# One weight load on all partitions, another gate and new planner constants in a fused attention and mixer kernel

## The chip, the core and the metric

The kernel runs on one core of one Trainium2 chip. Its engines have these names in the profile: PE is TensorE (matrix products), DVE is VectorE, ACT is ScalarE, POOL is GpSimd, and SP is SyncE, which here only starts transfers. Sixteen DMA engines move data between memory and the core. The metric is the device time of one execution in microseconds (us). A profiled execution shows a span, which is 1.7 to 1.9 us shorter than the time of the same execution; differences between spans are comparable with differences between times. Landings of transfers are taken from the landing records of a trace and stand 0.05 us later than the same events in the views.

One execution can differ from the next: each run lists the mean clock that was granted to PE, and a run that is over 1.5% longer than the fastest of its kernel is called slow and left out of comparisons. Ratios below are the mean time of one kernel's fast runs over the mean of the other's fast runs of the same rounds, so they are not quite the ratio of the medians that stand beside them. An interval in brackets is a 95% interval.

## The reference

The task is a gated linear attention, followed by a token mixing and a channel mixing layer, for 4 batches of 768 tokens with 8 heads of 48 (so 384 channels).

```python
# attention: per batch and head
f = 1.0 / (1.0 + np.exp(-f_logit))
for t in range(S):
    state = f[:, :, t, :, None] * state + np.einsum('bhd,bhe->bhde', k[:, :, t], v[:, :, t])
    y[:, :, t] = np.einsum('bhd,bhde->bhe', q[:, :, t], state)
# x = y with the heads side by side: (4, 768, 384)
xt = x.transpose(0, 2, 1)
h = np.maximum(xt @ w_tok1, 0.0) @ w_tok2      # (768, 256), (256, 768): token weights
u = x + h.transpose(0, 2, 1)
h2 = np.maximum(u @ w_ch1, 0.0) @ w_ch2        # (384, 1536), (1536, 384): channel weights
return u + h2
```

All inputs and the output are float32 in memory; the kernel multiplies in bf16.

## The kernel before

Each batch is treated in three parts of 256 tokens. A part is named by batch and number: "v of part 1,0" is the v data of batch 1, part 0. The program doesn't issue its instructions in the order in which they are written. A planner in the kernel file takes a list of operations with assumed durations, simulates the engines, and so fixes the order on each engine when the program is built. The assumed duration of a transfer is `xfer`. It never changes what a transfer costs on the chip, only the order that the planner chooses:

```python
            end = st + occ + lat
            if o.xfer is not None and e == "POOL":
                sw = max(st + occ + 1.5, sw) + o.xfer      # transfers that POOL starts
                pipe = max(pipe, st + occ) + o.xfer
                end = sw + 1.0
            elif o.xfer is not None:                       # transfers that SP starts
                pipe = max(st + occ + 0.9, pipe) + o.xfer
                # ... (cut)
```

The first token weight comes in four transfers of 64 partitions; two casts make it bf16. The channel weights are transferred by POOL, in halves a and b each. A gate is a tiny POOL copy that reads another load's data, so that the transfer behind it starts only when that load has landed:

```python
    gates = dict(zip(("wc1a", "wc1b", "wc2a", "wc2b"), ("w2s1", "-", "k1,1", "-")))
    # ...
        if at_ != "-":
            P.op(f"gate_{nm}", {"POOL": (0.13, 0.1)}, [at_], [],
                 lambda: nc.gpsimd.tensor_copy(gate_t, P[at_][:, 0, 0, 0:1]), -900 + len(sw), dep)
    # ...
    w1v = moe_w_tok1.rearrange("(kt p two) n -> two p kt n", p=64, two=2)
    # ...
    for n in range(2):
        def w1ld(n=n):
            for j in range(2):
                nc.sync.dma_start(out=flat(f"w1s{n}")[64 * j:64 * j + 64].rearrange("p (kt c) -> p kt c", c=DT),
                                  in_=w1v[j, :, 3 * n:3 * n + 3])
        P.op(f"w1l{n}", {"SP": (1.2, 0)}, [], [f"w1s{n}"], w1ld, -400 + n, [tail], xfer=0.393 / 0.35)
        # ... then one cast of 128x768 for each n, on POOL or ACT
```

Behind the token weights in SP's queue follow the loads of batch 1. The channel products are `ch1` (line L777, the first channel weight) and `ch2` (line L802, the second); in the changed kernel, and in kernels built from it without further lines, the same lines are L776 and L801. Filler matmuls (L858, later L857) on a dummy tile stand in PE's program before 40 us to keep PE busy while it would wait.

## Time and profile before

| quantity | before |
|---|---|
| time, median of three runs | 189.42 us (189.19 to 190.62) |
| span of the profiled run, clock | 186.9 us, 0.977 |
| PE busy | 173.3 us, 93% |
| PE at half clock, start excepted | 24.84 to 31.66 us, and from 185.3 us to the end |
| first channel matmul (L777) starts | 42.54 us |
| PE idle from 45 to 70 us | 25.00 - 22.94 = 2.06 us |
| PE idle from 70 to 140 us | 70.00 - 69.21 = 0.79 us |

The table is read in this way. PE is the bound, so the time can be cut up by PE alone: when the channel products begin, and how much PE stands idle after that. The last two rows come from the view that sums each engine's busy time over stretches. These are its rows for the kernel before. The columns are the stretch and its length, then for PE, PEld, DVE, ACT and POOL the busy time with the number of instructions, then the granted clock, the DMA share and the GB/s moved.

```profile
20.00:24.00 4.00, 3.26 (x94) 1.99 (x93) 2.88 (x6) 1.46 (x4) 2.81 (x3) 1.00 1.12 227
...
45.00:70.00 25.00, 22.94 (x336) 14.48 (x337) 17.50 (x32) 18.11 (x35) 11.31 (x17) 1.00 1.07 224
70.00:140.00 70.00, 69.21 (x941) 42.58 (x938) 46.95 (x85) 45.60 (x87) 25.90 (x39) 1.00 0.96 182
```

The last figure of the first row will matter: while the half loads of the first token weight began to move, the DMA engines delivered 227 GB/s.

### The profile page before, as it was taken

The numbers are of one execution on the slowest core, as the hardware profiler recorded it, in microseconds if no ns is written. First come the engines' busy times: TensorE is split into PE (matmuls) and PEld (weight loads), VectorE is DVE, ScalarE is ACT, GpSimd is POOL, SyncE is SP. The second block draws the span as 40 slices with busy tenths as digits, with TensorE's granted clock in tenths as the row PEclk, the third lists the DMA queues.
The fourth block names the chain that finished last, engine by engine and source line by source line (L and its number), as shares of the span: only waits on it lengthen the run. The fifth ranks groups of instructions, "written<-read, shape, count | busy, mean of one in ns | idle before, by whom it ended". The sixth has DMA issues, their size and how long they took to land.

```text
span 186.9 us, 5369 instructions
## 1 busy us (share of the span) xinstructions
PE 173.3 (93%) x2218; PEld 106.3 (57%) x2224; DVE 111.0 (59%) x213; ACT 117.3 (63%) x214; POOL 60.4 (32%) x97
## 2 busy tenths in 40 slices
PE   6699879999998799999999999999999999999990
PEld 2345555665566466666556655666557566665550
DVE  6389747699676487388866473979447173112021
ACT  3878479699988079578974854649516650833900
POOL 3017644373763311554562453024301130000000
PEclk9999966999999999999999999999999999999998
DMA  6999999999999979999999999305970003303033
GB/s 147 261 261 264 240 277 206 209 256 249 260 224 212 241 180 255 121 291 290 193 243 182 162 296 188 96 4 119 135 142 4 4 0 84 84 4 84 0 86 84
DMA packets 69592, 31.01 MB, mean 166 GB/s; under 512 B 63168, under 2 KB 69312, under 8 KB 69568
## 3 DMA queue, kind: packets, MB, share of 16 engines
q1 hardware_dynamic: 67200, 28.32, 73.0%
q0 software_dynamic: 2368, 2.36, 7.6%
q8 instruction: 17, 0.28, 0.6%
q14 instruction: 7, 0.06, 0.1%
HBM read 25.17 MB, written 4.72 MB: 160 GB/s over the span
## 4 chain that ended last, share of the span: by engine, by line
PE 69%; DMA 13%; ACT 6%; DVE 6%; issue 2%; POOL 2%; POOLq 0%; DVEq 0%; ACTq 0%
PE pp L802 24%; PE pp L777 20%; DMA w_ch<-in_moe_w_ch_dram 6%; PE pp L714 5%; DMA v_ld<-in_v_dram 4%; PE pp L730 3%; PE pp L662 3%; PE pp L674 3%; PE pp L645 3%; DMA f_ld<-in_f_logit_dram 2%; PE pp L858 2%; PE pp L600 2%; PE pp L751 2%; DVE xu L736 2%; DVE AmT L652 1%
## 5 line engine op out<-in xcount | busy, mean ns | idle before, releaser
L802 PE MATMUL pp<-w_ch,zT 128*128 128x384 bf16 x288 | 51.1, 326 | 1.9 <-DMA w_ch<-in_moe_w_ch_dram 1.9
L777 PE MATMUL pp<-uT,w_ch 128*128 128x384 bf16 x288 | 52.3, 326 | 0.2 <-ACT zT L784 0.2
L784 ACT ACTIVATE zT<-pp 128x384 bf16<-128x384 f32 x75 | 35.8, 492 | 21.6 <-PE pp L777 15.3
L802 PEld LDWEIGHTS <-zT 128*128 128x128 bf16 x288 | 27.1, 98 | 19.1 <-issue 2.1
L777 PEld LDWEIGHTS <-w_ch 128*128 128x128 bf16 x288 | 26.4, 98 | 16.9 <-issue 0.4
L812 DVE TENSOR_TENSOR xu<-xu,pp 128x384 f32<-128x384 f32 x24 | 13.2, 550 | 30.7 <-PE pp L802 30.7
L652 DVE TENSOR_TENSOR AmT<-pp,msk 128x1024 bf16<-128x1024 f32 x24 | 28.5, 1217 | 4.7 <-PE pp L645 3.4
L440 POOL CAST x_bf<-xu 128x768 bf16<-128x768 f32 x10 | 8.3, 829 | 29.5 <-ACT xu L698 29.5
L858 PE MATMUL pp<-idle 128*128 128x512 bf16 (+7 forms) x58 | 15.6, 382 | 2.2 <-DVE idle L340 1.5
L786 DVE TENSOR_SCALAR zT<-pp 128x384 bf16<-128x384 f32 x21 | 11.3, 553 | 7.4 <-PE pp L777 7.2
L557 POOL TENSOR_TENSOR qkh<-q_ld,G 128x384 bf16<-128x384 f32 x14 | 12.6, 914 | 7.2 <-ACT G L535 4.3
L440 POOL CAST v_bf<-v_ld 128x768 bf16<-128x768 f32 x10 | 8.3, 826 | 16.6 <-DMA v_ld<-in_v_dram 13.8
L494 ACT ACTIVATE f_ld<-f_ld 128x768 f32<-128x768 f32 x12 | 10.1, 838 | 5.6 <-DMA f_ld<-in_f_logit_dram 5.6
L501 DVE TENSOR_TENSOR Pf<-f_ld 128x384 f32<-128x384 f32 x12 | 7.1, 592 | 8.6 <-ACT f_ld L496 7.7
L698 ACT COPY xu<-pp 128x768 f32<-128x768 f32 x11 | 8.8, 798 | 5.3 <-PE pp L662 4.0
L736 DVE TENSOR_TENSOR xu<-xu,pp 128x384 f32<-128x384 f32 x24 | 11.5, 546 | 0.3 <-PE pp L730 0.2
L557 DVE TENSOR_TENSOR qkh<-k_ld,pp 128x384 bf16<-128x384 f32 x22 | 11.3, 546 | 0.6 <-ACT pp L537 0.6
L506 POOL TENSOR_TENSOR Plo<-Pf,Phi 128x384 bf16<-128x384 f32 x10 | 9.5, 946 | 5.4 <-ACT Phi L438 5.0
L645 PE MATMUL pp<-qkT 48*64 48x128 bf16 x384 | 9.9, 225 | 1.0 <-ACT qkT L438 0.4
L524 DVE TENSOR_TENSOR pp<-pp,f_ld 128x384 f32<-128x384 f32 x12 | 6.8, 563 | 6.9 <-PE pp L520 4.2
L535 ACT ACTIVATE G<-pp 128x768 bf16<-128x768 f32 x12 | 9.7, 808 | 1.2 <-DVE pp L524 1.0
L496 ACT ACTIVATE f_ld<-f_ld 128x768 f32<-128x768 f32 x12 | 10.2, 848 | 0.1
(83 smaller groups left out, 228.5 us busy)
## 6 DMA issues: line engine op xcount, KB each, us to landing
f_ld<-in_f_logit_dram SPq DMA_DIRECT2D x12, 384.0 KB, 6.3
q_ld<-in_q_dram SPq DMA_DIRECT2D x12, 384.0 KB, 6.4
k_ld<-in_k_dram SPq DMA_DIRECT2D x12, 384.0 KB, 6.3
v_ld<-in_v_dram SPq DMA_DIRECT2D x12, 384.0 KB, 6.4
out_dram<-xu SPq DMA_DIRECT2D x22, 192.0 KB, 2.7
w_ch<-in_moe_w_ch_dram POOLq DMA_DIRECT2D x4, 576.0 KB, 9.3
v_ld<-in_moe_w_tok_dram SPq DMA_DIRECT2D x4, 192.0 KB, 6.5
v_ld<-in_moe_w_tok_dram SPq DMA_DIRECT2D x1, 384.0 KB, 6.8
```

What stands on the lines that cost most here:

```text
L440: (nc.vector if e == "DVE" else nc.gpsimd).tensor_copy(o, x)
L496: lambda: nc.scalar.activation(f_(), f_(), AF.Ln, bias=1.0, scale=1.0), pg - 5.5)
L557: vec(e).tensor_tensor(o, x, g, ALU.mult)
L645: nc.tensor.matmul(A[64 * e:64 * e + 64, par, hp * 128:(hp + 1) * 128].rearrange("p (j t) -> p j t", j=2), lhsT=qkT(1, e)[rows, hp, j], rh ...
L652: lambda j=j: nc.vector.tensor_tensor(P[f"Am{j}{i}"], P[f"A{j}{i}"].rearrange("p b (a t) -> p (b a) t", t=128), msk[:, j].rearrange("p j t ...
L736: nc.vector.tensor_tensor(x, x, P[f"up{i}"][:, 0:DM], ALU.add)
L777: nc.tensor.matmul(pm, lhsT=w_ch1[:, kt, cc * 128:(cc + 1) * 128], rhs=uT[:, 3 * th:3 * th + 3, kt, :], start=(kt == 0), stop=(kt == 2))
L784: nc.scalar.activation(P[f"z{i}"], P[f"zp{i}"][:, 0:384], AF.Relu)
L786: nc.vector.tensor_scalar(P[f"z{i}"], P[f"zp{i}"][:, 0:384], 0.0, None, ALU.max)
L802: nc.tensor.matmul(P[f"op{i}"][:, 0:DM], lhsT=P[f"z{b},{th},{cc}"][:, c0:c0 + 128], rhs=w_ch2[:, cc, :], start=(cc == 0), stop=(cc == NCC ...
L812: nc.vector.tensor_tensor(x, x, P[f"op{i}"][:, 0:DM], ALU.add)
L858: nc.tensor.matmul(P.psum_tile[:, bank, 0:n], lhsT=idle[:, 0:128], rhs=idle[:, 0:n], start=True, stop=True)
```

## The change

It has three parts. The first token weight is loaded as pairs of rows on all 128 partitions in one transfer, and four casts of 64 partitions bring its rows to the partitions where they are needed. The gate of the second channel weight reads the landed q of part 1,1, no longer the k. And three constants of the planner say that POOL's transfers take 1.6 times as long, that DMA transposes take 1.3 us, not 1.1, and that stores take 1.7 us, not 1.1.

```diff
-                sw = max(st + occ + 1.5, sw) + o.xfer
+                sw = max(st + occ + 1.5, sw) + 1.6 * o.xfer
@@
-    gates = dict(zip(("wc1a", "wc1b", "wc2a", "wc2b"), ("w2s1", "-", "k1,1", "-")))
+    gates = dict(zip(("wc1a", "wc1b", "wc2a", "wc2b"), ("w2s1", "-", "q1,1", "-")))
@@
-    (two times two loads of 64 partitions, two casts of 128x768: shown above)
+    P.op("w1l", {"SP": (0.7, 0)}, [], ["w1s"], lambda: nc.sync.dma_start(
+        out=w1s.rearrange("p g two c -> p g (two c)"),
+        in_=moe_w_tok1.rearrange("(g p two) c -> p g (two c)", p=128, two=2)), -400, [tail], xfer=0.786 / 0.35)
+    tail = "~w1l"
+    for j in range(2):
+        for kk in range(2):
+            P.op(f"w1c{j},{kk}", {"POOL": pool_t(768), "ACT": act_t(768)}, ["w1s"], [f"w1{kk}"],
+                 lambda e, j=j, kk=kk: cast(
+                     e, w_tok1[64 * j:64 * j + 64].rearrange("p (g kk) c -> p kk g c", kk=2)[:, kk],
+                     w1s[64 * kk:64 * kk + 64, :, j]), T0 - LEAD - 4 + kk)
@@ (cut: priority of the second token weight; which weight half each matmul reads)
-                         P[f"qh{i}"][64 * e:64 * e + 64]), pr - 500, xfer=1.1)
+                         P[f"qh{i}"][64 * e:64 * e + 64]), pr - 500, xfer=1.3)
@@
-                     due(b, "o", tts[-1]) - 500, xfer=1.1 * len(tts) / 2)
+                     due(b, "o", tts[-1]) - 500, xfer=1.7 * len(tts) / 2)
```

More of the change, by code (lines that the diff above doesn't have):

```diff
@@ L396, in sw_dma @@
         sw.append(nm)
-    w1v = moe_w_tok1.rearrange("(kt p two) n -> two p kt n", p=64, two=2)
+    w1s = st([128, 3, 2, DT], FP32, "w1s")
     def flat(v):
@@ L402 @@
     for n in range(2):
-        P.value(f"w1s{n}", f"w1s{n}", "v")
         P.value(f"w2s{n}", f"w2s{n}", "vk"[n])
-    for n in range(2):
-        def w1ld(n=n):
-            for j in range(2):
-                nc.sync.dma_start(out=flat(f"w1s{n}")[64 * j:64 * j + 64].rearrange("p (kt c) -> p kt c", c=DT),
-                                  in_=w1v[j, :, 3 * n:3 * n + 3])
-        P.op(f"w1l{n}", {"SP": (1.2, 0)}, [], [f"w1s{n}"], w1ld, -400 + n, [tail], xfer=0.393 / 0.35)
-        tail = f"~w1l{n}"
-        P.op(f"w1c{n}", {"POOL": pool_t(768), "ACT": act_t(768)}, [f"w1s{n}"], [f"w1{n}"],
-             lambda e, n=n: cast(e, w_tok1[:, 3 * n:3 * n + 3].rearrange("p kt c -> p (kt c)"), flat(f"w1s{n}")),
-             T0 - LEAD - 4)
+    P.op("w1l", {"SP": (0.7, 0)}, [], ["w1s"], lambda: nc.sync.dma_start(
[8 more added lines that the diff above has]
+                     w1s[64 * kk:64 * kk + 64, :, j]), T0 - LEAD - 4 + kk)
     for kt in range(2):
@@ L417 @@
              lambda kt=kt: nc.sync.dma_start(out=flat(f"w2s{kt}"), in_=moe_w_tok2[128 * kt:128 * kt + 128]),
-             -398 + kt, [tail], xfer=0.393 / 0.35)
+             -390 + kt, [tail], xfer=0.393 / 0.35)
         tail = f"~w2l{kt}"
@@ L715, in tok1 @@
                                      rhs=P[f"xb{b},{kt // 2}"][:, kt % 2], start=(kt == 0), stop=(kt == NCH - 1))
-                ins = [f"xb{b},{kt // 2}", f"w1{kt // 3}"] + ([f"{g},{kt - 1}"] if kt else [f"xb{b},{first // 2}"])
+                ins = [f"xb{b},{kt // 2}", f"w1{kt % 2}"] + ([f"{g},{kt - 1}"] if kt else [f"xb{b},{first // 2}"])
                 P.op(f"tok1{b},{rt},{kt}", {"PE": (0.165, PE_LAT)}, ins, [f"{g},{kt}"], tok1, due(b, "tok1", kt))
```

## The prediction

> **What bounds the kernel now.** I read the page first (engine totals, then the 40 slices), then the chain of waits in order of time, then the timelines of TensorE (PE), GpSimd (POOL) and ScalarE (ACT) between 20 and 72 us, then the landings of the loads, and last the order of instructions per engine in both kernels.
>
> ```profile
> PE 173.3 (93%) x2218; PEld 106.3 (57%) x2224; DVE 111.0 (59%) x213; ACT 117.3 (63%) x214; POOL 60.4 (32%) x97
> ...
> PE   6699879999998799999999999999999999999990
> ...
> PEclk9999966999999999999999999999999999999998
> DMA  6999999999999979999999999305970003303033
> ```
>
> Each digit is 4.67 us. PE is the bound: busy 93%, and from about slice 15 (70 us) to the last slice nearly without a hole. From there on only matrix work that disappears, or starts earlier, moves the end. What is left to win is in the holes before 70 us: the fill of the first batch (to 42.5 us, where the first channel matmul L777 starts), a stretch at half clock in slices 5 and 6, and two holes at 58 and 62 us. The timeline of PE shows the last two:
>
> ```profile
> 57.14 0.37 PE L662 MATMUL pp<-v_bf,AmT 64*128 64x48 bf16 x16
> 58.08 3.09 PE L802 MATMUL pp<-w_ch,zT 128*128 128x384 bf16 x18 [0.57 <-DMA w_ch<-in_moe_w_ch_dram]
> 62.47 3.09 PE L802 MATMUL pp<-w_ch,zT 128*128 128x384 bf16 x18 [1.31 <-DMA w_ch<-in_moe_w_ch_dram]
> ```
>
> Each half of the second channel weight is waited for: 0.57 + 1.31 = 1.88 us. The chain of waits says why it is late:
>
> ```profile
> 48.71 0.91 POOL qkh L557
> 49.62 0.07 POOL gate_t L393
> 49.69 0.87 POOL w_ch L433
> 50.57 11.86 DMA w_ch<-in_moe_w_ch_dram
> 62.47 3.09 PE pp L802 x18
> ```
>
> The gate copy (L393) reads the landed k of batch 1, part 1. By the landing records that load is down at 47.17, so at 49.62 the gate was not waiting for data: it stood in POOL's queue behind a state cast and a q product, which themselves waited for VectorE (DVE).
>
> **What the Trainium skill says.** "DMA: Bandwidth & Descriptors", section "Rules for kernel authors", advises against splitting a transfer over two disjoint partition halves, since both halves use the same 16 engines, and for one transfer of 128 partitions. That is the first part of this change. The trace agrees in direction: the four 192 KB half loads of the first token weight landed at 24.12, 25.13, 26.09 and 27.11, about 1.0 us each, or 2.0 us per 384 KB, where full 128-partition loads of 384 KB landed every 1.5 us before 18 us, and the two of the second token weight (3 KB runs) took 0.8 and 1.1 us. The same page, section "Issuing engines are not separate DMA queues", says that transfers started by POOL and by SP share the same engines. The trace agrees: while the channel weights moved (52 to 62 us), the f load between them landed at 61.62, 6.9 us after the one ahead of it (54.68), against 1.3 to 1.5 us for loads around 45 to 50 us. "TensorE: Matmul & The Clock Gate", section "Part 1: The HAM clock gate (the \"warmup\" mystery)", gives half clock after an idle window of about 3.4 us. The trace has half clock from 24.84 to 31.66 us (6.82 us, about two such windows), after only a 1.19 us hole at 24 us, so low activity seems to be enough.
>
> **The change, part by part.**
>
> 1. *Load of the first token weight.* Four loads of 64 partitions (1 KB runs) become one load of 128 partitions (2 KB runs). Last landing before: 27.11, and v ahead of it at 23.41, so 3.70 us for 768 KB. Estimate after: 2 x (1.1 to 1.5) = 2.2 to 3.0 us, so a landing near 26.0. Its first half was usable at 25.13 before, now nothing is before 26.0. Loads behind it come 0.7 to 1.5 us earlier. SP also issues one transfer, not four (4.60 us by its timeline, much of it queue pressure); that is not on the path.
>
> 2. *Casts.* Two casts of 128x768 (908 ns on POOL, 832 ns on ACT) become four of 64x768, two on each. Half the partitions do not halve the time: POOL took 353 ns for 64x192, about 500 for 128x384 and 829 for 128x768, a line in the elements per partition alone. So POOL and ACT each pay about 0.85 us more. With the landing at 26.0 they end at 26.0 + 2 x 0.87 = 27.8 us; before they ended at 26.1 and 28.0. In program order the first token matmuls now stand behind the first-part state and value products, near 28.6 us, so they shouldn't wait. Against this, ACT hands one transpose eviction (1.00 us at 27.87, stuck behind a cast that waited 1.19 us) to DVE, which can do it at 26.1. The mask (L652 at 31.15) and what follows may be ready some 0.3 to 0.7 us earlier.
>
> 3. *But PE there runs in order and is full.* From 25.09 to 36.15 us, where the last four token matmuls of batch 0 begin, PE has only about 0.4 us of holes, because filler matmuls (L858) are part of its program:
>
> ```profile
> 34.63 1.51 PE L858 MATMUL pp<-idle 128*128 128x512 bf16 x7 [0.16 <-issue]
> 35.99 0.81 PE L714 MATMUL pp<-x_bf,w_tok 128*128 128x384 bf16 x4
> ```
>
> By the order of instructions the fillers in this stretch even grow by 448 columns (6208 to 6656), at 217 ns for 512 warm some 0.19 us. So of the earlier data only about 0.4 - 0.2 = 0.2 us reaches the first channel matmul.
>
> 4. *First channel weight.* Its gate (second token weight landed, 29.01 before) opens about 1 us earlier, so it lands near 36.5 and 40, not 37.41 and 40.95. L777 starts at 42.5 on the u chain (six adds L736, 2.89 us), so this is worth 0.
>
> 5. *Second channel weight.* The gate now reads q of batch 1, part 1, landed at 45.81 before and near 45.0 after. More important, in POOL's new order nothing stands between the small glast product (42.92 before) and the gate: the state cast and the q products come later or go to DVE. So the issue moves from 49.69 to about 45.3, 4.4 us earlier. With the same 8.4 and 11.9 us from issue to landing (58.09 - 49.69; 62.48 - 50.57) the halves land near 53.7 and 58.1. PE asks for the first at 57.5 - 0.87 (two groups moved behind it) - 0.2 = 56.4, and for the second near 61, since three L777 blocks (1.5 us) are put ahead of the second halves. Spare time: 2.7 and about 3 us, so both waits go: 1.88 us.
>
> 6. *Model constants* (slower POOL transfers, DMA transposes and stores) change only the order. From 66 us on the kernel before has about 1 us of holes (0.38 at 85.7, 0.20 at 108.5, some tenths near 111); I take the same after.
>
> Sum: 1.88 + 0.2 = 2.1 us off 189.42, so 187.3 us.
>
> **The rivals.**
>
> *A new wait takes the place of the old one.* Loads of q, k, v for part 2 of batch 1 (49.83, 51.95, 53.43) and two f loads now move beside the second channel weight. Its 2 halves displace roughly three loads, so v of part 2 may land near 57 and the second f near 61. The transposes of that part are due near 64.5 us, with the gated q at about 63.8 on POOL and k at 64.3 on DVE by their orders: margins of only 0.3 to 0.7 us. For it: ACT now has two f exponentials ahead of an eviction, so a late f stalls it. Against it: the same bytes are down by 62 us in either order. If it happens, 0.5 to 1.5 us of the gain go back: 188 to 189 us.
>
> *Evictions become the bound.* Between 40 and 50 us ACT is busy 9.55 and DVE 8.73 of 10 us; DVE gets two q products (2 x 0.55 us) from POOL. Against it: L777 waited only 0.2 us in all for an eviction. Cost if it happens, 0.3 to 1 us.
>
> *The clock.* If the changed arrivals let PE be busier in the window before 28.25, half clock ends one window (3.4 us) earlier, worth up to 1.7 us of PE time; that would give about 185.6. If PE stands waiting for the later first cast and stays slow one window more, it loses as much: 189. For no change: the first 633 rows of PE's program are identical, so the hole at 24 us that goes before the slow stretch, set by the landing of v at 23.41, stays.
>
> *Hidden anyway.* If another engine held PE back right behind 62 us, the 1.88 us would return as waits. Against it: L777 and L802 from 65.9 to 85 us show no hole over 0.2 us.
>
> **Range and chances.** Before 70 us some 3.5 us of holes can be won at most without the clock, so 2% (3.8 us, under 185.6) needs nearly all of them or the clock: 0.08. Slower by 2% needs several rivals at once: 0.03. The reordering of the later stages may move the end by about 1 us either way, which sets the range: 185.7 to 189.1.
>
> **What would show it.** Right: one load for the first token weight landing near 26; four 64x768 casts near 0.85 us each; the second channel weight issued near 45.5 and no hole before L802 that ends on a DMA; L777 starting at 42.0 to 42.5; the half clock still some 6.8 us. Wrong: L802 still waiting for a landing; a new hole at 58 to 67 us before transposes or scores; half clock of another length; or holes above 2 us in all between 70 and 180 us.

## The result, and the profile after

The changed kernel took 183.49 us in the median of four runs (183.16 to 186.49; the last is a slow one), beside 189.31 us of the kernel before (four runs). The ratio of the fast runs is 0.9715 [0.9635, 0.9795]. It is faster by 5.8 us, where 2.1 had been predicted.

The page of the changed kernel has these lines. In the first is the busy time of each engine with its share of the span, then come busy tenths of PE in 40 slices of 4.54 us, the granted clock, and the DMA engines.

```profile
PE 170.7 (94%) x2216; PEld 104.6 (58%) x2222; DVE 115.4 (64%) x220; ACT 115.0 (63%) x208; POOL 61.5 (34%) x98
...
PE   6899878989999999999999999999999999999990
...
PEclk9999999999999999999999999999999999999998
DMA  6999999999999999999999899429640003303033
```

The slices at half clock are gone, and PE is full from slice 10 on. What this cost or gained is not to be read from it; the experiments below ask that. The timeline of PE shows the milestones (start, duration, instruction; a bracket at the end would give an idle time before it and what ended that):

```profile
39.75 0.65 PE L776 MATMUL pp<-uT,w_ch 128*128 128x384 bf16 x3
...
54.33 2.11 PE L801 MATMUL pp<-w_ch,zT 128*128 128x384 bf16 x12
...
56.68 1.15 PE L801 MATMUL pp<-w_ch,zT 128*128 128x384 bf16 x6
...
58.20 1.62 PE L776 MATMUL pp<-uT,w_ch 128*128 128x384 bf16 x9
59.66 3.09 PE L801 MATMUL pp<-w_ch,zT 128*128 128x384 bf16 x18
```

The first channel matmul starts at 39.75 us, 2.79 us earlier than the 42.54 of before. None of the second weight's matmuls has a bracket: both waits are gone. Between its halves the planner has put three groups of L776. The sums over stretches say the same, and what happens later:

```profile
20.00:24.00 4.00, 2.87 (x93) 1.89 (x92) 2.93 (x5) 2.83 (x6) 2.75 (x4) 1.00 0.95 342
...
45.00:70.00 25.00, 24.81 (x369) 15.70 (x368) 19.21 (x34) 18.16 (x34) 11.44 (x19) 1.00 1.13 233
70.00:140.00 70.00, 69.93 (x1000) 43.63 (x998) 50.74 (x91) 42.46 (x82) 26.43 (x38) 1.00 0.91 170
```

PE's idle time from 45 to 70 us fell from 2.06 to 0.19 us, and from 70 to 140 us from 0.79 to 0.07 us. The account of the profiled pair is therefore 2.79 (earlier start of the channel products) + 1.87 + 0.72 = 5.4 us, of 186.9 - 181.4 = 5.5 us. The prediction had the second term, almost none of the first, and nothing of the third.

The first term has a trace in the casts. These are ACT's lines for the v of part 0,2, which is loaded just ahead of the token weight, and for the weight. First the kernel before:

```profile
23.38 0.83 ACT L438 CAST v_bf<-v_ld 128x768 bf16<-128x768 f32 x1 [1.80 <-DMA v_ld<-in_v_dram]
...
27.14 0.83 ACT L438 CAST w_tok<-v_ld 128x768 bf16<-128x768 f32 x1 [1.19 <-DMA v_ld<-in_moe_w_tok_dram]
```

Then the changed kernel:

```profile
21.97 0.83 ACT L437 CAST v_bf<-v_ld 128x768 bf16<-128x768 f32 x1 [0.40 <-DMA v_ld<-in_v_dram]
...
24.43 1.69 ACT L437 CAST w_tok<-w1s 64x768 bf16<-64x768 f32 x2
```

Two casts of 64x768 take 1.69 us, 0.85 each, as predicted. But the v *ahead* of the weight was usable 1.4 us earlier, which the prediction had not thought of. The load of the weight landed at 24.01 us; the last of the four half loads had landed at 27.11.

The third view is the chain of waits, the path that ended last, here around the start of the channel products of the changed kernel (start, duration, what):

```profile
27.87 11.86 DMA v_ld<-in_v_dram
39.78 0.84 POOL v_bf L439
...
40.66 0.44 PE pp L599 x32
```

A transfer carries the path there: the v of part 1,0, issued at 27.87 and landed at about 39.78 us. Before, it had landed at 42.07. This v is needed at 40.66, behind the first three channel matmuls. Ahead of those, PE's program has transposes of a product that DVE makes of another load, the k of part 1,0; it landed at 38.27 us (40.71 before), and PE waited 0.23 us for that product at 38.95. The last view is POOL's timeline at the gate of the second channel weight in the changed kernel:

```profile
43.35 0.19 POOL L393 COPY gate_t<-q_ld 128x1 f32<-128x1 f32 x1 [2.58 <-DMA q_ld<-in_q_dram]
43.47 1.70 POOL L432 DMA_DIRECT2D w_ch<-in_moe_w_ch_dram  x2
```

POOL stood 2.58 us before the gate with nothing to do, so now it is really the landing that opens it. The halves landed at 51.58 and 55.92 us, before PE asked for them at 54.33 and 59.66.

### The profile page after: what moved, and what is told of

Read it like the earlier page. It is cut to its first block, busy times and chain, and to the rows that moved or that the text cites. A ratio compares the mean times of both kernels' runs of the same rounds, so it can differ in the third digit from the quotient of the medians.

```text
span 181.4 us, 5357 instructions
## 1 busy us (share of the span) xinstructions
PE 170.7 (94%) x2216; PEld 104.6 (58%) x2222; DVE 115.4 (64%) x220; ACT 115.0 (63%) x208; POOL 61.5 (34%) x98
## 4 chain that ended last, share of the span: by engine, by line
PE 73%; DMA 9%; DVE 8%; ACT 6%; issue 2%; POOL 0%; DVEq 0%; ACTq 0%
PE pp L801 25%; PE pp L776 23%; DMA v_ld<-in_v_dram 7%; PE pp L661 4%; PE pp L713 3%; PE pp L673 3%; PE pp L644 3%; PE pp L599 2%; PE pp L729 2%; DVE qkh L556 2%; DMA f_ld<-in_f_logit_dram 2%; PE pp L576 2%; PE pp L857 2%; PE pp L750 1%; DVE xu L735 1%
## 5 line engine op out<-in xcount | busy, mean ns | idle before, releaser
L776 PE MATMUL pp<-uT,w_ch 128*128 128x384 bf16 x288 | 52.2, 326 | 0.0
L801 PE MATMUL pp<-w_ch,zT 128*128 128x384 bf16 x288 | 51.8, 326 | 0.0
L783 ACT ACTIVATE zT<-pp 128x384 bf16<-128x384 f32 x69 | 33.1, 491 | 19.8 <-PE pp L776 19.7
L801 PEld LDWEIGHTS <-zT 128*128 128x128 bf16 x288 | 27.0, 98 | 16.6
L776 PEld LDWEIGHTS <-w_ch 128*128 128x128 bf16 x288 | 26.3, 98 | 16.4 <-issue 0.2
L785 DVE TENSOR_SCALAR zT<-pp 128x384 bf16<-128x384 f32 x27 | 14.1, 553 | 7.8 <-PE pp L776 6.9
L439 POOL CAST v_bf<-v_ld 128x768 bf16<-128x768 f32 x10 | 8.6, 858 | 22.1 <-DMA v_ld<-in_v_dram 18.8
L644 PE MATMUL pp<-qkT 48*64 48x128 bf16 x384 | 9.1, 220 | 1.7 <-DVE state L624 1.0
L857 PEld LDWEIGHTS <-idle 128*128 128x128 bf16 x62 | 5.7, 105 | 7.9 <-issue 3.6
```

Of the source, the lines that this page charges most:

```text
L439: (nc.vector if e == "DVE" else nc.gpsimd).tensor_copy(o, x)
L644: nc.tensor.matmul(A[64 * e:64 * e + 64, par, hp * 128:(hp + 1) * 128].rearrange("p (j t) -> p j t", j=2), lhsT=qkT(1, e)[rows, hp, j], rh ...
L776: nc.tensor.matmul(pm, lhsT=w_ch1[:, kt, cc * 128:(cc + 1) * 128], rhs=uT[:, 3 * th:3 * th + 3, kt, :], start=(kt == 0), stop=(kt == 2))
L783: nc.scalar.activation(P[f"z{i}"], P[f"zp{i}"][:, 0:384], AF.Relu)
L785: nc.vector.tensor_scalar(P[f"z{i}"], P[f"zp{i}"][:, 0:384], 0.0, None, ALU.max)
L801: nc.tensor.matmul(P[f"op{i}"][:, 0:DM], lhsT=P[f"z{b},{th},{cc}"][:, c0:c0 + 128], rhs=w_ch2[:, cc, :], start=(cc == 0), stop=(cc == NCC ...
```

## The experiments

The question was where the 3.7 us came from that the prediction lacked. The theories were these. **Load**: four half loads slow all that moves around them, and the first channel matmul waits for those landings. **Clock**: the half clock at 24.84 us, which vanished, had cost the time. **Gate**: the earlier issue of the second channel weight takes its waits away. **Order**: the planner's constants, not the gate, take the waits and the later holes away. All sixteen kernels gave correct results. The kernel before ran beside them in each of four groups; its median there was 189.3 us (e1 to e4), 189.46 (e5 to e8), 190.49 (e9 to e12) and 190.63 (e13 to e16).

### e1: the kernel before, unchanged

No edit. It shows the scatter, and whether the half clock comes by chance in some executions and not in others (chance theory).

> The kernel before, unchanged, to see how often its clock drops. Chance theory (the half clock between 24.8 and 31.7 us[...]): of its runs some have a mean clock near 0.977 and some near 0.995, the latter about 2 us faster (187 to 188 against 189 to 190.5). Cause theory (the old load order itself makes the clock drop): all runs near 0.977 and none under 188.5.

The median was 189.17 us of 14 runs (187.74 to 191.66), ratio 0.9992 [0.9955, 1.0029]. The profiled run (190.38 us) had half clock for 10.24 us, from 24.66 to 34.90, and its first channel matmul came at 44.07, 1.53 us later than in the other profile of the same kernel. So a long stretch at half clock does cost something. Whether the usual one does is the next question. The times already speak against it: among all 98 runs of this kernel, the seven with a mean clock of 0.976 to 0.978 (0.977 was that of the profile with the usual stretch) have a median of 188.82 us, and the 27 fast ones at 0.994 or more have 188.81. The longer stretch does show: four fast runs at 0.972 or 0.973 took 189.6 to 190.61 us. So of the chance theory the spread of clocks came true, but not the 2 us.

### e2: the kernel before with the new load alone

```diff
 # before, plus: one load on 128 partitions, four casts of 64x768, the priority of the second token weight
 # gate k1,1 and the three old constants stay
```

> The kernel before with the new load and casts of the first token weight alone; old gate, old model constants. The order of instructions is that of before but for some 30 moved ones. Load theory (one whole load brings the second token weight down 2.9 us earlier, 26.1 for 29.0, and with it the first channel matmul 2.8 us earlier): 186.3 to 187.0, first channel matmul at 39.5 to 40.5, and the waits of about 1.9 us for the second channel weight still there. Gate theory (my prediction: the load is worth 0.2 us and the gate 1.9): 189.0, first channel matmul at 42 to 42.5.

The median was 186.93 us of 6 runs (186.14 to 187.84), ratio 0.987 [0.9821, 0.9918]. The first channel matmul came at 40.24 us, 2.30 earlier than before. But PE's timeline shows that part of it was lost again at once:

```profile
55.72 3.08 PE L801 MATMUL pp<-w_ch,zT 128*128 128x384 bf16 x18 [0.51 <-DMA w_ch<-in_moe_w_ch_dram]
61.21 3.09 PE L801 MATMUL pp<-w_ch,zT 128*128 128x384 bf16 x18 [2.41 <-DMA w_ch<-in_moe_w_ch_dram]
```

PE waited 0.51 + 2.41 = 2.92 us for the second channel weight, 1.04 more than before: PE was there earlier than the weight was. The load is worth much more than the 0.2 us that the prediction gave it, and its worth depends on the other parts.

### e3: the changed kernel with the old load

```diff
 # after, with the four loads of 64 partitions and two casts of 128x768 of before
```

> The changed kernel with the old four half loads and two casts of the first token weight; new gate and constants kept. Load theory: first channel matmul back at 42 to 42.5, no wait for the second channel weight, 186 to 186.8 in runs without the clock drop. Gate theory: 183.5 to 184, first channel matmul at 40. If the old load also brings back the clock drop: mean clock near 0.977 in most runs, 187.5.

The median was 186.32 us of 6 runs (186.19 to 187.09), ratio 0.9847 [0.9798, 0.9895]. In its profile PE had full clock through the whole program until 183.6 us. All the same the first channel matmul came at 42.45 us. So the half loads set that time with or without half clock. PE's idle time was small, 25.00 - 24.87 = 0.13 us from 45 to 70 us and 0.18 us from 70 to 140.

### e4: the kernel before with PE kept busy at 24 us

```diff
+    fillers.setdefault("trq0,2,1", []).extend([(bank, 512)] * 4)   # four dummy matmuls before the transposes at 24 us
```

> The kernel before with four more filler matmuls of 512 columns (0.87 us) in TensorE's hole at 24 us, nothing else. Clock theory (the hole before 24.84 is what drops the clock): mean clock 0.995 in nearly all runs, 187.0 to 187.8, first channel matmul 1.2 to 2 us earlier (near 41). If the clock is not what holds that stretch, or the drop is not due to the hole: within 0.3 us of the kernel before run beside it.

The median was 189.67 us of 22 runs (187.65 to 192.62), ratio 0.9992 [0.9962, 1.0022]. The half clock at 24.8 us was gone in the profile (which fell in a slow run, with a stretch at half clock of its own only from 61 us; what lies ahead of that is used here). The last token matmuls of batch 0 started at 34.70 us, 1.3 earlier than before, but the first channel matmul still came at 42.36. The timelines of DVE and PE show what PE was waiting for, and that of POOL what came right behind:

```profile
40.96 1.02 DVE L557 TENSOR_TENSOR qkh<-k_ld,pp 128x384 bf16<-128x384 f32 x2 [1.31 <-DMA k_ld<-in_k_dram]
...
41.57 0.40 PE L577 MATMUL pp<-ident,qkh 128*128 128x128 bf16 x4 [1.29 <-DVE qkh L557]
...
42.78 0.83 POOL L440 CAST v_bf<-v_ld 128x768 bf16<-128x768 f32 x1 [2.15 <-DMA v_ld<-in_v_dram]
```

The k of part 1,0 landed at 40.9 us, and PE transposes the product that DVE makes of it (L577) ahead of the first channel matmul. The v of the same part landed at 42.7, behind that matmul, and held PE for another 0.65 us. e3's profile has the same waits, 1.27 and 0.54 us. The clock theory falls here for the usual stretch of 6.8 us: with the slow stretch taken out, loads held the same point.

### e5: the changed kernel, its load split over partition halves

```diff
-    nc.sync.dma_start(out=w1s..., in_=...)
+    for j in range(2):
+        r = slice(64 * j, 64 * j + 64)
+        nc.sync.dma_start(out=w1s[r]..., in_=...[r])       # runs of 2 KB as in the change
```

> The changed kernel with its one load cut into two of 64 partitions each, runs of 2 KB kept; order of all else unchanged. If writing half the partitions is what made the old loads slow: the token weights land as in the kernel before (v ahead of them at 23.3, second token weight at 28.5 to 29), first channel matmul at 42, 185.5 to 186. If the 1 KB runs were the cause: landings within 0.3 us of the changed kernel (22.0 and 26.1), 183.5.

The median was 186.71 us of 6 runs (185.23 to 188.0), ratio 0.9869 [0.9811, 0.9926]. This gives the load's gain back. The window of 4 us in which this load begins reads:

```profile
20.00:24.00 4.00, 3.52 (x97) 2.03 (x94) 2.93 (x5) 1.17 (x4) 2.81 (x3) 1.00 1.02 226
```

The rate is 226 GB/s, as in the kernel before (227) and not as after (342). The v ahead landed at 23.7 us, the v of part 1,0 at 42.2, and the first channel matmul came at 42.66. None of its runs was at full clock (the profile has half clock from 24.85 to 31.67 again), so its time alone would not decide; the landings do.

### e6: the changed kernel, two loads with runs of 1 KB

```diff
+    for j in range(2):
+        nc.sync.dma_start(out=w1s[:, :, j],                 # all 128 partitions, but runs of 1 KB
+                          in_=moe_w_tok1.rearrange("(g p two) c -> two p g c", p=128, two=2)[j])
```

> The changed kernel with its one load cut into two of all 128 partitions each, in runs of 1 KB (the even rows, then the odd rows). If half the partitions were the cause: landings near those of the changed kernel (22.0 and 26.1 to 26.5), 183.5 to 184. If the run length was the cause: second token weight at 28.5 to 29, first channel matmul at 42, 185.5 to 186.

The median was 184.96 us of 6 runs, 184.15 of the four fast ones, ratio 0.9736 [0.9675, 0.9796]. Its profiled span, 181.4 us, is that of the changed kernel. The same window:

```profile
20.00:24.00 4.00, 3.49 (x96) 2.00 (x94) 2.89 (x6) 2.52 (x6) 2.84 (x3) 1.00 1.03 304
```

With two transfers and the short runs of before, but all partitions, the rate was 304 GB/s, the v ahead landed at 22.3 us, and the first channel matmul came at 39.34. So neither the number of transfers nor the run length is what mattered. Half the partitions is.

### e7: the changed kernel with the old gate

```diff
-("w2s1", "-", "q1,1", "-")
+("w2s1", "-", "k1,1", "-")
```

> The changed kernel with the second channel weight gated on k of batch 1, part 1, again; new load and constants. Gate theory (the gate alone removes the wait): the gate stands again behind the q products of GpSimd, waits for the second channel weight of 1.5 to 3 us come back, 185.5 to 186.5. If the model constants removed it (by putting other matmuls ahead): waits under 0.5 us, 183.5 to 184.2.

The median was 184.83 us of 6 runs (183.27 to 187.1), 183.94 of the five fast ones, ratio 0.9751 [0.9687, 0.9814]. With the old gate the second channel weight was issued at 46.88 and its halves landed at 55.2 and 59.6 us, some 3.6 us later than in the changed kernel. PE did not wait for either:

```profile
54.57 2.12 PE L776 MATMUL pp<-uT,w_ch 128*128 128x384 bf16 x12
56.53 3.09 PE L801 MATMUL pp<-w_ch,zT 128*128 128x384 bf16 x18
...
60.88 0.65 PE L776 MATMUL pp<-uT,w_ch 128*128 128x384 bf16 x3
```

Four groups of L776 stand ahead of the first L801. Given the new constants, the gate is not needed. At full clock (0.994 and above) the three runs of e7 had a median of 183.53 us and those of the changed kernel 183.49, so no worth of the gate can be told from zero.

### e8: the changed kernel with the old constants

```diff
-                sw = max(st + occ + 1.5, sw) + 1.6 * o.xfer
+                sw = max(st + occ + 1.5, sw) + o.xfer
 # and 1.3 -> 1.1 for the transposes, 1.7 -> 1.1 for the stores
```

> The changed kernel with the old model constants; new load and gate. If the gate alone is enough: no wait for the second channel weight, and 183.5 to 184.2. If the constants are what lays out the later stages without holes (0.8 us of holes between 70 and 140 us before, under 0.1 after): 184.2 to 185 with those holes back.

The median was 187.84 us of 22 runs (186.44 to 191.74), ratio 0.9921 [0.9891, 0.9951]. The gate was the new one, and the issue was early (44.28 us), yet PE waited:

```profile
54.12 1.64 PE L801 MATMUL pp<-w_ch,zT 128*128 128x384 bf16 x9 [0.49 <-DMA w_ch<-in_moe_w_ch_dram]
...
58.56 1.62 PE L801 MATMUL pp<-w_ch,zT 128*128 128x384 bf16 x9 [1.39 <-DMA w_ch<-in_moe_w_ch_dram]
```

That is 1.88 us, the sum of before. The planner asked for each half earlier, and the halves landed later (54.1 and 58.6 us) than in the changed kernel (51.6 and 55.9). The holes after 70 us grew to 70.00 - 68.67 = 1.33 us. So the order theory stands against the gate theory.

### e9 and e10: the changed kernel again, and with its hole at 22.5 us filled

```diff
 # e9: no edit
+# e10: fillers.setdefault("sc0,1,1", []).extend([(bank, 512)] * 4)
```

> The changed kernel, unchanged, to see its spread beside the next three. If the clock drop depends on where the window falls: runs between 183.2 and 187.5, the fast ones with a mean clock of 0.995 or more. If the changed kernel is free of it: all runs within 183 to 184.

The median of e9 was 183.6 us of 6 runs (182.78 to 184.26), ratio 0.9677 [0.9629, 0.9726]. The result repeats. In its profile (184.04 us) PE waited 0.82 us for k of part 1,0, landed at 39.1, and started the channel products at 40.60: they still hang on that landing.

> The changed kernel with four more filler matmuls of 512 columns in TensorE's hole of 0.95 us at 22.5 us, all else in the same order. Now the first channel matmul is set by TensorE's own chain and no longer by loads alone, so if low activity there is what drops the clock, fewer runs lie above 185 and the median falls 0.5 to 1.5 us below the unchanged one beside it. If not: medians within 0.3 us of each other.

The median of e10 was 184.13 us of 6 runs (183.34 to 186.31), ratio 0.9706 [0.9648, 0.9764], so not faster. In its profile PE waited 1.82 us for the product that DVE makes of k of part 1,0, and the channel products began at 41.69. Keeping PE busy there buys nothing.

### e11, e12, e15 and e16: can the landings be moved further up?

Each moves the first channel weight behind loads of batch 1, since those loads now set the start of the channel products.

```diff
+# e11: gates ("w2s1", "k1,0", "q1,1", "-")
+# e12: gates ("q1,0", "-", "q1,1", "-")
+# e15: e11 with P.by_name["gate_wc1b"].after += ("~lo1,1",)
+# e16: e15 without two fillers before the last token matmuls of batch 0
```

> The changed kernel with the second half of the first channel weight gated on the landing of k of batch 1, part 0. In the changed kernel that load (38.3) and v (39.8) land only after both halves (34.3, 37.8), and the value product waits 0.26 us for v. Load theory: k and v land near 36 and 37.5, first channel matmul at 39.2 to 39.5, 183 us; if the later gate holds back GpSimd or the second half comes late, a wait for it near 43 to 46 us and 184 to 185.

The median was 184.87 us (184.35 to 184.99), ratio 0.9743 [0.9699, 0.9787]. The k and v of part 1,0 did land at 35.7 and 37.2 us, some 2.6 earlier. But POOL's gate now stood before other work, PE waited 0.88 us for a product of POOL at 37 us and 0.98 us more at 86.8, and the first channel matmul came at 40.96. A limit directly behind took over.

> The changed kernel with the first channel weight gated on q of batch 1, part 0 (30.7) and not on the second token weight (26.1). k and v of that part land near 33 to 35, but the first half of the channel weight only near 38.6 to 39.5, about when TensorE asks for it (39.75). If loads of k and v were the limit: 182.5 to 183.3. If the channel weight becomes the limit: a wait of 0.5 to 1.5 us before the first channel matmul, 184 to 185.

The median was 186.57 us (185.87 to 190.46), ratio 0.9831 [0.9778, 0.9884]. The k and v landed at 32.5 and 33.9 us. But the first channel weight itself came too late: its first half landed at 41.5 us, after the 39.75 at which the changed kernel begins to use it, and the channel products began at 42.70, behind other work of PE.

> As the run with the second half of the first channel weight gated on k of batch 1, part 0, but with the gate placed behind GpSimd's second low-part product (the 0.88 us hole at 37 us in that run came from it). k and v still land near 36 and 37.5, the hole goes, first channel matmul at 39.5 to 40: 183.8 to 184.3, for that order has a hole of 0.98 us at 86 us that stays. If that hole goes too, 182.8.

> The kernel of the run before, with two of the eight filler matmuls ahead of the last four token matmuls of batch 0 taken out (0.43 us of TensorE's program). With loads and channel weights early, TensorE's own chain should be the limit, so 0.2 to 0.4 us faster than the run before. If loads or vector work hold it: the same.

The medians were 184.33 us (184.0 to 185.37) for e15 and 184.32 us (183.7 to 185.59) for e16, ratios 0.9734 [0.9681, 0.9786] and 0.974 [0.9681, 0.98]. In e15's profile the first channel matmul came only at 41.38, behind a wait of 1.56 us for a product of POOL. In e16's it came at 39.69, as in the changed kernel, though k and v had landed at 35.3 and 36.8. In e11, e15 and e16 PE is idle 1.1 us from 70 to 140 us. None of these beats the changed kernel, and no version in this study does.

### e13 and e14: which constant does what

```diff
-# e13: 1.6 * o.xfer  ->  o.xfer            (the other two constants new)
-# e14: 1.3 -> 1.1 and 1.7 -> 1.1           (the factor 1.6 kept)
```

> The changed kernel with one constant put back: the planner's transfers issued by GpSimd at 1.0 instead of 1.6 times their time; the two others new. If this constant is what puts first-layer channel matmuls ahead of the second-layer ones: waits of 1 to 2 us for the second channel weight, 185.5 to 187.5. If the transpose and store constants do it: no such wait, 183.5 to 184.

> The changed kernel with the two other constants put back (transposes 1.1, stores 1.1) and the 1.6 for transfers issued by GpSimd kept. If the 1.6 alone matters: no wait for the second channel weight, 183.5 to 184.2. If the two others lay out the later stages: 184.5 to 186, with holes of 0.5 to 1 us between 70 and 140 us.

The median of e13 was 184.72 us of 6 runs (184.08 to 186.57), ratio 0.977 [0.9705, 0.9836]; that of e14 186.98 us of 6 runs (185.85 to 188.69), ratio 0.9854 [0.9791, 0.9917]. The sums over stretches show two different losses. First e13:

```profile
45.00:70.00 25.00, 22.39 (x295) 13.61 (x294) 16.30 (x31) 14.05 (x27) 10.43 (x16) 1.00 1.04 222
70.00:140.00 70.00, 69.81 (x1017) 43.66 (x1016) 50.78 (x91) 43.59 (x82) 29.17 (x43) 1.00 0.91 176
```

Then e14:

```profile
45.00:70.00 25.00, 24.83 (x370) 15.70 (x368) 19.27 (x34) 18.18 (x34) 11.45 (x18) 1.00 1.13 240
70.00:140.00 70.00, 67.83 (x948) 41.90 (x946) 46.59 (x85) 42.34 (x82) 26.78 (x40) 1.00 0.87 169
```

Without the factor of POOL's transfers (e13), PE is idle 2.61 us from 45 to 70 us: it waits 0.93 and 1.34 us for the second channel weight again. Without the constants of the transposes and stores (e14), it is idle 0.17 us there but 2.17 us from 70 to 140 us, of which 1.42 us stand before one token product at 113 us. The profiled runs took 186.57 and 185.85 us, so beside the 183.16 of the changed kernel the idle time explains most of both differences (2.5 of 3.4, 2.1 of 2.7). The profiled run of e13 was the longest of its six, though; four of them lay between 184.08 and 184.77, so the waits must often be shorter than the profile shows.

### All parts together

Each row is a profiled run, apart from the last column. "Idle" is the length of the stretch less PE's busy time. The landings are those of the v of part 0,2 and of the k and v of part 1,0.

| kernel | load | gate | constants | v 0,2 | k 1,0 | v 1,0 | first channel matmul | idle 45 to 70 | idle 70 to 140 | median of fast runs |
|---|---|---|---|---|---|---|---|---|---|---|
| before | old | old | old | 23.4 | 40.7 | 42.1 | 42.54 | 2.06 | 0.79 | 189.06 |
| e2 | new | old | old | 22.2 | 38.7 | 40.2 | 40.24 | 2.93 | 0.73 | 186.94 |
| e3 | old | new | new | 23.2 | 41.0 | 42.7 | 42.45 | 0.13 | 0.18 | 186.32 |
| e7 | new | old | new | 22.0 | 38.1 | 39.4 | 39.58 | 0.00 | 0.64 | 183.94 |
| e8 | new | new | old | 22.1 | 38.9 | 40.2 | 40.77 | 2.11 | 1.33 | 187.82 |
| e13 | new | new | POOL's old | 22.2 | 38.4 | 39.8 | 39.90 | 2.61 | 0.19 | 184.72 |
| e14 | new | new | POOL's new only | 22.3 | 38.2 | 40.0 | 39.72 | 0.17 | 2.17 | 186.92 |
| after | new | new | new | 22.0 | 38.3 | 39.8 | 39.75 | 0.19 | 0.07 | 183.53 |

The times of before and after here are over the 73 fast runs of before in the four groups and e1, and over the nine of after, with e9. In this table the load decides when the first channel matmul starts (up to 1 us of scatter, as e9's 40.60 shows), and POOL's constant decides the first idle column. The second is small only where the gate and the constants of the transposes and stores are all new.

## Why the prediction was wrong

It said 187.3 us and gave 0.08 to faster by over 2%. Measured were 183.49 us and 2.85% by the ratio. Its own steps, one after the other:

**Step 1, the load: half right, and the missed half mattered.** One load, landing later than v and earlier than the last half load, was right; 26.0 was said and 24.01 measured. The step took v's landing (23.41) as fixed and added the weight's transfer behind it. But the transfers of one queue are in flight together: v was issued ahead and yet landed 1.4 us earlier once the half loads behind it were gone (22.00), and 1.2 to 1.7 us later again whenever they were back (e3 23.2, e5 23.7). "Loads behind it come 0.7 to 1.5 us earlier" was 2.9 us for the second token weight (29.01 to 26.12), 2.4 for k of part 1,0 (40.71 to 38.27) and 2.3 for v (42.07 to 39.78).

**Step 2, the casts: right.** About 0.85 us for each of the four, and PE did not wait for the weight.

**Step 3, "PE there runs in order and is full": the step that failed.** It let only 0.2 us of the earlier data reach the first channel matmul. It was 2.8 us in the profiled pair, and 2.1 to 2.8 us in time: e2 gained 2.1 us on before (189.06 to 186.94), and the changed kernel stands 2.8 below e3 (186.32 to 183.53). The reading had two faults. PE was full between 25.09 and 36.15 us in that profile, but 6.6 of those 11 us passed at half clock, so a busy PE there was no proof of a bound; e4 and e3 ran the stretch at full clock, with the last token matmuls of batch 0 at 34.70 and 34.82 us, against 35.99. And those runs show the second limit that then appears: k of part 1,0 lands at 40.9 to 41.0, and PE waits 1.3 us for the product that DVE makes of it, so the first channel matmul comes at 42.4 although those token matmuls ran more than a microsecond earlier. PE and the loads were two limits of nearly the same length, and the chain of waits names only one. With the new load both came earlier. Two smaller readings of the step were off as well: 36.15 us is where the fillers end, while the token matmuls begin at 35.99, and the fillers between the transposes (25.09 before, 24.28 after) and those matmuls did not grow by 448 columns; the traces have 4992 before and 4928 after.

**Step 4, the first channel weight is worth 0: right in itself**, as far as a landing at 34.26 us instead of 37.41 was followed by no use of it before 39.75; in e12 it landed at 41.5, and that was too late.

**Step 5, the second channel weight: right result, but the gate doesn't decide it.** The issue moved from 49.69 to 43.47 us (45.3 was said), the landings to 51.58 and 55.92, and both waits went, 1.87 us against 1.88. The halves lay ready 2.75 and 3.74 us before PE asked for them (2.7 and about 3 had been said), so for the changed kernel itself the sum was sound. But e7 loses the same waits with the old gate, and e8 and e13 keep waits of 1.88 and 2.27 us with the new one. What decides is the order that the planner makes when it is told that POOL's transfers are slower. In e13 PE asked for the halves at 53.02 and 57.00 us, in the changed kernel at 54.33 and 59.66, because one more group of L776 stands ahead of the first half and four more ahead of the second, with some products of batch 1. Had the halves landed as late as in e13 (53.95 and 58.34), that order would still not have waited. The step did mention such groups, as spare time, not as the cause. Putting the constants back costs 4.3 us (e8, 187.82 against 183.53), more than the waits of the kernel before. With the old constants the new gate shortens the waits from 2.92 (e2) to 1.88 us (e8), but the time is not shorter (186.94 and 187.82).

**Step 6, "model constants ... change only the order": right as a description and wrong as a price.** The step took the same 1 us of holes after 66 us. They nearly vanished: 0.79 to 0.07 us from 70 to 140 us. The new constants of transposes and stores are needed for that (without them 2.17 us stay in e14), and so is the new gate (with the old one 0.64 us stay in e7). Which of these two constants it is was not tried.

**The rivals.** The new wait from the loads of part 1,2 did not come, and evictions did not become the bound (idle 0.19 us). The clock did change in the profile, and it is tempting to book 1.7 us for it, as the rival did. It isn't the cause. Among the 98 runs of the kernel before (e1 and the four groups), 27 fast ones were at a clock of 0.994 or above, with a median of 188.81 us; eight such runs of the changed kernel had 183.49. At full clock the difference is thus 5.32 us, nearly the whole. Only the longer stretch (10.24 us in e1's profile) shows a cost.

**The sum.** At full clock the load alone gives 188.81 - 186.75 (e2) = 2.1 us, the gate and constants alone 188.81 - 186.20 (e3) = 2.6 us, and both 5.3 us: some 0.6 us more than the sum of the two. This rest is smaller than the intervals of the ratios (about 0.9 us either way). It would fit that the load's gain is partly waited away in e2 without the new order, which is an argument from e2's longer wait (2.92 us against 1.88), not a run of its own. The gate alone and the constants alone were not tried on the kernel before. Still open is why the halves of the second channel weight land some 2.5 us later in e8 and e13 than in the changed kernel, though their issue differs by only 0.5 to 0.8 us.

## What to carry to other kernels

A busy engine in front of a milestone is no proof that the milestone hangs on it: look at what clock it was busy, and list the landings that the milestone needs, since a second limit of nearly the same length doesn't show in the chain. A transfer that uses the DMA engines badly delays also what was issued ahead of it and all that is queued behind, so price it by the loads around it rather than by its own landing. In a kernel with a planner, constants of its model are part of the schedule, and a change of them is to be priced like a change of code.

## What the Trainium skill lacked or had wrong

- "DMA: Bandwidth & Descriptors", section "Rules for kernel authors", advises against two transfers to disjoint partition halves because they serialize and gain nothing. The advice held, but the section doesn't say that they cost: 226 and 227 GB/s over 20 to 24 us with half loads (e5 and before), 304 and 342 GB/s with all partitions (e6 and after), and some 2.6 us of time in this kernel (e5 with 186.72 us in the median of its fast runs, e6 with 184.15). That is not lacking in the skill as a whole: "SBUF — State Buffer", section "Door 1: The DMA port swizzle (why `[64,N]` ≈ `[32,N]`)", has 64 partitions reach only half of the ports and move fewer bytes per second than 128. The rates here agree in direction; whether ports are the reason, no run here shows.
- No page that was looked up says what such a load does to its neighbours in the same queue: the load issued ahead of it landed 1.4 us later (23.41 against 22.00).
- "TensorE: Matmul & The Clock Gate", section "Part 1: The HAM clock gate (the "warmup" mystery)", gives an idle window of about 3.4 us as the cause of half clock; here no window of that length was idle. (A later section of that page does allow for short idle times.) Half clock began at 24.84 us although PE's longest wait there was 1.19 us and it was busy 3.26 of the 4 us from 20 to 24; the same program had none of it in other runs (those at a mean clock of 0.994 and above). Nor is little work there enough, as the prediction guessed: the changed kernel's PE was busy only 2.87 us of the same 4 and kept full clock. A stretch of 6.8 us had little cost in time, since loads held the same point (e4); one of 10.24 us came with a start of the channel products 1.53 us later (e1).
